# Pairing heads across the two groups on the partitions: landmark logits as 64-row, 32-column tiles, one scale for all heads

## Chip, cores, metric

One core of one Trainium2 chip. The metric is the device time of one execution in microseconds (us). The kernel before took 1018.75 us, the median of three runs.

## What is computed

Two stages. The first is landmark (Nystrom) attention with 8 batches, 8 heads, 576 tokens, 64 dimensions and 32 landmarks a head, the landmarks being means of 18 tokens:

```python
q_lm = q.reshape(B, H, 32, 18, D).mean(axis=3)      # k_lm the same from k
A  = softmax(scale * q    @ k_lm.T)                 # 576 x 32 a head
Bm = softmax(scale * q_lm @ k_lm.T)                 # 32 x 32
C  = softmax(scale * q_lm @ k.T)                    # 32 x 576
Z = Bm.T / (norm1(Bm) * norminf(Bm) + 1e-6)         # norms over the whole matrix
for _ in range(6): Z = 2 * Z - Z @ Bm @ Z
attn = A @ Z @ C @ v
```

The second takes x (batch, token, 512 columns of all heads), adds the real part of its two-dimensional Fourier transform over tokens and columns (u = x + mixed), normalises each token, and computes out = u + relu(un @ w_ch1) @ w_ch2 with 2048 hidden columns. All inputs are float32, w_ch1 and w_ch2 float64.

## The kernel before

Three threads of one program are woven into one order by a scheduler written out in the kernel (`run`, L930). Each thread is a Python generator that yields how long it wants to wait on a clock of estimates (`self.now`); whichever thread of the highest priority is due emits its next instructions. TensorE's order is thereby fixed by hand; the other engines' orders are left to the framework's scheduler, which goes by the order of emission and by free buffers. `attention` (priority 1) goes through the eight batches, `weights` (2) decodes the float64 weights and splits each into two fp16 halves, `mlp` (3) fills the rest: for each chunk of 256 tokens 192 hidden-layer matmuls (tile h) and 96 of the second layer (tile acc). Where nothing is due early on, filler matmuls are issued (L954).

Products that need more than fp16 are made as three fp16 matmuls (`mm3`: high x high, high x low, low x high) from a `split` of the operand (ScalarE writes the high half, VectorE the low). Small products stay in fp32.

The heads of a batch stand in two groups g of four. `load` (L360) brings k and q of group g as a tile of 128 partitions (two heads of 64 dimensions) by two pairs r. `tokens` (L382) sums the landmarks (lm), takes bounds of |q| and |k|, sets a scale for each group, and makes the logits of A: for each group a unit of four token tiles (u = 0, 1) and one unit (u = 2) for 64 remaining tokens. Since two heads share the 128 rows, each matmul's other operand (kbd) carries two heads' landmarks side by side with zeros in the wrong half (`mask2`). Softmax, the transposes of A, and the sums and differences over the heads of a group (F1, F2, Fh), which the transform needs, follow. `landmarks` (L536) is spawned as soon as lm is there. It makes the logits of B and C from the masked landmarks of q (qbd): for each group and pair an fp32 matmul of 128 rows by 64 columns, 32 columns wide for B (L551) and twice 288 wide for C (L589). Then come B's softmax and norms (nrm), the transposed C times v, six rounds of the iteration (RE, E), and the factors for `mix` (L725), which adds everything into u, from which `norm` and the MLP go on.

Four PSUM banks (`ps_at`, tile name at) serve all of the attention's matmuls in turn; `till(..., banks=n)` (L201) holds a thread back until the estimates say that n of them are free. SyncE issues all DMAs.

Of the kernel before, what the change touches and what calls it, by code (L numbers as in the profile page):

```python
# [131 lines left out]
class Kernel:  # L132
# [227 lines left out]
    def load(self, b):  # L360
# [4 lines left out]
        for g in range(2):  # L365
            kf, qf = self.big(), self.big()
            gs = slice(2 * g, 2 * g + 2)
            nc.sync.dma_start(kf[:, 0 : 2 * S].rearrange("p (r t) -> p r t", r=2), self.k[b, :, gs])
            nc.sync.dma_start(qf[:, 0 : 16 * SEG].rearrange("p (r t) -> p r t", r=2), self.q[b, :, gs])
# [12 lines left out]
    def tokens(self, b, st):  # L382
# [6 lines left out]
        lm = sm.tile([P, 2, 128], F32, name="lm", bufs=1)  # L389
        am = self.small(4, "amax")  # L390
        qbd = sm.tile([P, 4, 64], F32, name="qbd", bufs=1)
        qhs = []
        for g in range(2):
            kf, qf = loads[g][0][:, 0 : 2 * S], loads[g][1][:, 0:NQ]
            first = V.tensor_reduce(lm[:, g, 64:128], kf.rearrange("p (m t) -> p m t", t=18), AX.X, ALU.add)
# [3 lines left out]
            lv = lm[:, g, 0:64].rearrange("p (x o m) -> p x o m", o=2, m=8)  # L399
# [6 lines left out]
            A.activation(qhs[g][:, 0:NQ], qf, AF.Abs, accum_out=am[:, g : g + 1])  # L406
# [7 lines left out]
        st["loads"], st["qbd"], st["lm"] = loads, qbd, lm  # L414
        self.spawn(self.landmarks(b, st))

        eq, rq = self.power(am[:, 0:2], 2, 2.0**-13, "aq", b == 1)
        kb = self.small(2, "kb", BF16)
        V.tensor_tensor(kb, am[:, 2:4], eq, ALU.mult)
        yield self.till(kb, more=AM)  # L420
        ek, rk = self.bound(kb, 2, 2.0**-13, "ak")
        sc = self.small(4, "sc")
        V.tensor_tensor(sc[:, 0:2], eq, rk, ALU.mult)
        V.tensor_scalar(sc[:, 2:4], ek, 1.0 / 144.0, None, ALU.mult)
# [4 lines left out]
        for h2 in range(2):  # L429
            ms, cols = self.mask2[:, h2 : h2 + 1], slice(32 * h2, 32 * h2 + 32)  # L430
            V.tensor_scalar(
                kbd[..., cols].rearrange("p g y r m -> p (g y r) m"), klm.rearrange("p g y (r m) -> p (g y r) m", r=2),
                ms, None, ALU.mult,
            )
        qm = [h[:, 0:2048].rearrange("p (y r t) -> p y r t", y=2, r=2) for h in qhs]
        qr = [h[:, 2048:2304].rearrange("p (y r t) -> p y r t", y=2, r=2) for h in qhs]
        for g in range(2):
            qs = loads[g][1][:, 0:NQ].rearrange("p (x t) -> p x t", t=2 * SEG)
            for t, a, w in ((qm[g], 1, 128), (qr[g], 129, 16)):
                split(  # L440
                    *(t[:, y].rearrange("p r (s t) -> p (r s) t", t=w) for y in range(2)),
                    qs[:, :, a : a + w], rq[:, g : g + 1],
                )
            if g == 0:
                yield self.till(qhs[0], kbd)
# [3 lines left out]
        scr = self.small(1, "scr")  # L449
        for g in range(2):  # L450
            V.tensor_copy(scr[64 * g : 64 * g + 64], sc[64 * g : 64 * g + 64, 2 + g : 3 + g])
        aes = []
        for u in range(3):
            yield self.till(qhs[min(u, 1)])
            ps = self.psum()
            nh, scA = (16, sc[:, 2 + u : 3 + u]) if u < 2 else (4, scr)
            for j in range(4) if u < 2 else range(2):
                rows, at, g = (slice(0, P), 128 * j, u) if u < 2 else (slice(64 * j, 64 * j + 64), 0, j)
                for pr in range(2):
                    mm3(ps[rows, at + 64 * pr : at + 64 * pr + 64],  # L460
                        lambda y: qm[g][:, y, pr, 128 * j : 128 * j + 128] if u < 2 else qr[g][:, y, pr],
                        lambda y: kbd[:, g, y, pr, :])
# [7 lines left out]
            A.activation(ae, ae, AF.Exp, scale=scA)  # L470
# [7 lines left out]
        for u in range(3):  # L478
# [18 lines left out]
            if u < 2:  # L497

                F1, F2 = self.mid()[:, 0:512], self.mid()[:, 0:512]
                for x, op in enumerate((ALU.add, ALU.subtract)):  # L500
                    V.tensor_tensor(F1[:, 256 * x : 256 * x + 256], ae[:, 0:256], ae[:, 256:512], op)
                f1 = F1.rearrange("p (x k m) -> p x k m", x=2, k=2)
                for x, op in enumerate((ALU.add, ALU.subtract)):
                    (V if x == 0 else G).tensor_tensor(
                        F2[:, 256 * x : 256 * x + 256].rearrange("p (x m) -> p x m", x=2), f1[:, :, 0], f1[:, :, 1], op
                    )
            else:
                Fs.append(hl)
                break
            Fh = self.mid().bitcast(F16)[:, 0 : 2 * w].rearrange("p (y t) -> p y t", y=2)  # L510
            A.copy(Fh[:, 0], F2)
            G.tensor_tensor(Fh[:, 1], F2, Fh[:, 0], ALU.subtract)
            Fs.append(Fh)
        CS = self.big().bitcast(F16).rearrange("p (g y x t) -> p g y x t", g=2, y=2, x=2)
        for x in range(2):
            yield self.till(*Fs, banks=2)
            pss = [self.psum(), self.psum()]
            for g in range(2):
                for o in range(2):
                    i = (3, 0)[o] if x == 0 else (1, 2)[o]  # L520
                    mm3(pss[g][:, 160 * o : 160 * o + 160], lambda y: Fs[g][:, y, 128 * i : 128 * i + 128],
                        lambda y: self.t1[:, i, y, :], start=(o == 0), stop=False)
# [13 lines left out]
    def landmarks(self, b, st):  # L536
# [3 lines left out]
        loads, qbd, lm = st["loads"], st["qbd"], st["lm"]  # L540
# [11 lines left out]
        V.tensor_scalar(Bd.rearrange("p g m -> p (g m)"), ps[:, 0:64], 1.0 / 2592.0, None, ALU.mult)  # L552
# [23 lines left out]
        while b == 1 and self.seconds < NF // 2 - HB:  # L576
            yield 0.5

        for g in range(2):
            kv = loads[g][0][:, 0 : 2 * S].rearrange("p (r t) -> p r t", r=2)  # L580
# [443 lines left out]
```

## Time and profile before

| | |
|---|---|
| median of three runs | 1018.75 us (1017.17 to 1018.84) |
| profiled execution | 1018.43 us |
| its span, first to last instruction | 1016.6 us |
| TensorE busy | 969.0 us, 8407 matmuls |
| VectorE, ScalarE, POOL busy | 608.2, 335.5, 125.9 us |
| mean granted TensorE clock | 0.98 |

The profile shows one execution. Busy time of TensorE is pipelined, so matmul durations overlap; how long a piece of its stream takes is read from the start of its first instruction to the start of the next piece. An fp32 matmul of the program stands as two records. Batches are told apart by their first logits: B of batches 0 to 7 starts at 9.1, 131.4, 218.5, 326.2, 450.4, 555.1, 662.2 and 788.9 us.

### The profile page before, as it was taken

Reading aid. Unit: us, or ns where it says so; the run is one execution under the profiler, and the core shown is the slowest. Engines: PE = TensorE matmul, PEld = TensorE weight load, DVE = VectorE, ACT = ScalarE, POOL = GpSimd, SP = SyncE. Lnnn points to the kernel's source line nnn. Section 1 sums busy time; section 2 is a strip of 40 time slices with the busy share of each in tenths; the row PEclk is TensorE's granted clock in tenths of the full one; section 3 lists DMA queues with packets and bytes.
Section 4 is the critical chain, followed back from the end, with each engine's and each line's share of the span. In section 5 each row is a group of like instructions: output and inputs, shape, how many; then the busy total and the mean of one; then the engine's idle time right before and its main releaser. Section 6 shows DMA issues by size and latency. Waiting matters only on the chain.

```text
span 1016.6 us, 20320 instructions
## 1 busy us (share of the span) xinstructions
PE 969.0 (95%) x8407; PEld 673.3 (66%) x8407; DVE 608.2 (60%) x1654; ACT 335.5 (33%) x723; POOL 125.9 (12%) x144
## 2 busy tenths in 40 slices
PE   5776989999999999999999999999999999999998
PEld 3654756667776676666766776667676676666665
DVE  6979797786655855287556855686453834351111
ACT  4658653343223322142233323332212322111110
POOL 0000000013011400024011401122020220110000
PEclk8887999999999999999999999999999999999999
DMA  9863204142312240112402240225020200120000
GB/s 328 254 250 111 83 2 167 22 71 51 148 21 45 43 164 11 43 36 53 161 12 53 50 168 6 58 48 180 1 53 11 58 15 22 22 53 21 1 22 21
DMA packets 97772, 74.63 MB, mean 73 GB/s; under 512 B 68112, under 2 KB 86544, under 8 KB 97552
## 3 DMA queue, kind: packets, MB, share of 16 engines
q1 hardware_dynamic: 97680, 73.34, 24.7%
q8 instruction: 66, 1.08, 0.5%
q14 instruction: 26, 0.21, 0.1%
HBM read 48.02 MB, written 9.44 MB: 57 GB/s over the span
## 4 chain that ended last, share of the span: by engine, by line
PE 82%; DVE 11%; ACT 3%; DMA 2%; issue 1%; POOL 1%; SPq 0%; DVEq 0%; POOLq 0%; ACTq 0%
PE h L210 34%; PE acc L210 34%; PE at L210 13%; DVE w L127 2%; DVE mid L127 1%; ACT mid L127 1%; DMA mid<-mid 1%; DVE lm L127 1%; DVE cmx L127 1%; DVE asum L127 1%; DMA big<-q_dram 1%; DMA big<-k_dram 1%; POOL mid L127 1%; PE at L215 1%; DVE amx L127 0%
## 5 line engine op out<-in xcount | busy, mean ns | idle before, releaser
L210 PE MATMUL h<-unT,w 128*128 128x256 f16 x3456 | 411.2, 273 | 0.0
L210 PEld LDWEIGHTS <-w 128*128 128x128 f16 (+1 forms) x3584 | 346.2, 99 | 73.2 <-issue 3.3
L210 PE MATMUL acc<-w,h 128*128 128x512 f16 x1680 | 394.3, 380 | 0.0
L210 PEld LDWEIGHTS <-h 128*128 128x128 f16 x1680 | 161.8, 98 | 161.9 <-issue 4.4
L127 DVE SCALAR_TENSOR_TENSOR h<-h 128x512 f16<-128x512 f32 x140 | 96.1, 687 | 198.7 <-ACT h L127 198.0
L127 ACT ACTIVATE h<-h 128x512 f16<-128x512 f32 x140 | 83.2, 595 | 308.0 <-PE h L210 295.8
L127 POOL TENSOR_TENSOR r<-ve,mhalf 128x2 f32<-128x2 f32 (+1 forms) x20 | 13.7, 685 | 411.1 <-DVE ve L127 404.1
L127 POOL TENSOR_TENSOR mid<-mid 128x640 f16<-128x640 f32 (+2 forms) x36 | 40.9, 1144 | 114.2 <-ACT mid L127 107.9
L127 DVE TENSOR_TENSOR mid<-mid 128x256 f32<-128x256 f32 (+2 forms) x68 | 45.3, 682 | 13.2 <-DMA mid<-mid 9.4
L127 DVE TENSOR_REDUCE lm<-big 128x32 f32<-128x576 f32 (+1 forms) x48 | 44.2, 946 | 10.2 <-DMA big<-k_dram 9.5
L127 DVE SCALAR_TENSOR_TENSOR u<-at,scw,row 128x128 f32<-128x128 f32 (+3 forms) x120 | 38.6, 389 | 13.8 <-PE at L210 11.8
L210 PEld LDWEIGHTS <-big 128*128 128x128 f16 (+1 forms) x768 | 39.7, 101 | 10.2 <-issue 2.8
L210 PEld LDWEIGHTS <-mid 64*128 64x128 f16 (+1 forms) x624 | 30.0, 96 | 18.8 <-issue 8.6
L127 ACT CAST row<-row 128x512 f16<-128x512 f32 (+1 forms) x40 | 20.7, 551 | 62.7 <-DVE row L127 62.7
L127 DVE SCALAR_TENSOR_TENSOR row<-at,scw,row 128x262 f32<-128x262 f32 (+1 forms) x48 | 21.3, 486 | 28.3 <-ACT row L127 21.4
L127 POOL TENSOR_TENSOR row<-row 128x512 f16<-128x512 f32 (+1 forms) x33 | 34.3, 1055 | 30.7 <-ACT row L127 28.8
L210 PE MATMUL at<-RE,E 128*128 128x96 f32 (+1 forms) x192 | 30.5, 281 | 4.3 <-DVE RE L127 4.3
L127 DVE SCALAR_TENSOR_TENSOR u<-acc,wsc,u 128x512 f32<-128x512 f32 x36 | 26.8, 749 | 12.5 <-PE acc L210 11.8
L210 PEld LDWEIGHTS at<-RE,E 128*128 128x128 f32 x192 | 27.1, 194 | 10.6 <-DVE RE L127 4.4
L210 PE MATMUL at<-mid,big 128*128 128x262 f16 (+1 forms) x288 | 31.8, 279 | 0.0
L127 DVE SCALAR_TENSOR_TENSOR big<-big,aq_r 128x1024 f16<-128x1024 f32 (+1 forms) x32 | 26.8, 868 | 3.9 <-ACT big L127 3.9
L127 ACT CAST mid<-mid 128x512 f16<-128x512 f32 (+1 forms) x28 | 18.1, 671 | 28.2 <-POOL mid L127 20.5
(166 smaller groups left out, 928.6 us busy)
## 6 DMA issues: line engine op xcount, KB each, us to landing
w<-w_dram SPq DMA_DIRECT2D x22, 512.0 KB, 8.7
big<-v_dram SPq DMA_DIRECT2D x16, 640.0 KB, 8.9
big<-q_dram SPq DMA_DIRECT2D x16, 584.0 KB, 6.0
big<-k_dram SPq DMA_DIRECT2D x16, 576.0 KB, 5.0
out_dram<-u SPq DMA_DIRECT2D x36, 256.0 KB, 2.0
big<-w_dram SPq DMA_DIRECT2D x10, 512.0 KB, 6.8
t<-t_dram SPq DMA_DIRECT2D x1, 1048.0 KB, 9.2
unT<-row SPq DMA_TRANSPOSE x64, 2.5
```

Source lines behind the costliest of these rows:

```text
L127: return call(out, *args, **kw)
L210: self.nc.tensor.matmul(out, a, b, start=start, stop=stop, skip_group_check=True)
L215: self.nc.tensor.transpose(out, a, ident)
```

## The change

Heads are paired across the groups: partitions 0 to 63 carry the heads of group 0, 64 to 127 those of group 1; the four heads of a group stand as two tiles e by two columns o. Each tile of k or q now comes by two DMAs of 64 partitions. One scale serves all heads. Landmarks of q need no mask: a head's B and C are matmuls of its own 64 rows by 32 columns, so eight small tiles cover the array, and both groups' B and C go into four banks, B behind the first half of C. The remaining 64 tokens of A become 24 matmuls of 32 columns in place of 12 of 64. The sums over heads are taken between the two units of A, and so stand behind both.

```diff
 load():
-            gs = slice(2 * g, 2 * g + 2)
-            nc.sync.dma_start(kf[...], self.k[b, :, gs])
-            nc.sync.dma_start(qf[...], self.q[b, :, gs])
-            for t in (kf, qf):
+            for t, src, n in ((kf, self.k, S), (qf, self.q, 8 * SEG)):
+                for half in range(2):
+                    nc.sync.dma_start(
+                        t[64 * half : 64 * half + 64, 0 : 2 * n].rearrange("p (o t) -> p o t", o=2),
+                        src[b, :, 2 * half + g].rearrange("(o p) t -> p o t", o=2),
+                    )
 tokens():
-            for h2 in range(2):
-                ms, cols = self.mask2[:, h2 : h2 + 1], slice(32 * h2, 32 * h2 + 32)
-                V.tensor_scalar(
-                    qbd[:, 2 * g : 2 * g + 2, cols], lm[:, g, 0:64].rearrange("p (r m) -> p r m", r=2), ms, None, ALU.mult
-                )
-            yield self.till(qbd)
-        V.tensor_reduce(am[:, 2:4], lm[:, :, 64:128], AX.X, ALU.max, apply_absolute_value=True)
+            yield self.till(lm)
+        V.tensor_reduce(km, lm[:, 1].rearrange("p e m -> p (e m)"), AX.X, ALU.max, apply_absolute_value=True)
...
-        eq, rq = self.power(am[:, 0:2], 2, 2.0**-13, "aq", b == 1)
+        V.tensor_tensor(qs, am[:, 0:1], am[:, 1:2], ALU.add)
+        eq, rq = self.power(qs, 1, 2.0**-13, "aq", b == 1)
...
-        for g in range(2):
-            split(klm[:, g, 0], klm[:, g, 1], lm[:, g, 64:128], sc[:, g : g + 1])
+        split(*(klm[:, y].rearrange("p e m -> p (e m)") for y in range(2)), lm[:, 1].rearrange("p e m -> p (e m)"), sc[:, 0:1])
...
-        scr = self.small(1, "scr")
-        for g in range(2):
-            V.tensor_copy(scr[64 * g : 64 * g + 64], sc[64 * g : 64 * g + 64, 2 + g : 3 + g])
...
+            if u < 2:
+                pt = ps.rearrange("p (j g r m) -> p j g r m", j=2, g=2, r=4)
+                for j in range(2):
+                    for r in range(4):
+                        at = 128 * (2 * u + j)
+                        mm3(pt[:, j, :, r], lambda y: qm[r // 2][:, y, r % 2, at : at + 128], lambda y: kbd[:, y, r // 2, r % 2].rearrange("p (g m) -> p g m", g=2))
+            else:
+                for r in range(4):
+                    for g in range(2):
+                        mm3(ps[64 * g : 64 * g + 64, 32 * r : 32 * r + 32], lambda y: qr[r // 2][:, y, r % 2],
+                            lambda y: kbd[:, y, r // 2, r % 2, 32 * g : 32 * g + 32])
...
+        F1 = [self.mid()[:, 0:512] for _ in range(2)]
+        for x, op in enumerate((ALU.add, ALU.subtract)):
+            V.tensor_tensor(F1[x], aes[0], aes[1], op)
+        for x, op in enumerate((ALU.add, ALU.subtract)):
+            F2 = self.mid()[:, 0:512]
+            for k in range(2):
+                (V if x == 0 else G).tensor_tensor(F2[:, 256 * k : 256 * k + 256], F1[k][:, 0:256], F1[k][:, 256:512], op)
 landmarks():
-        ps = self.psum()
-        for g in range(2):
-            for pr in range(2):
-                mm(ps[64 * pr : 64 * pr + 64, 32 * g : 32 * g + 32], qbd[:, 2 * g + pr], lm[:, g, 64 + 32 * pr : 96 + 32 * pr])
+        yield self.till(lm, banks=4)
+        heads = [(slice(64 * g, 64 * g + 64), slice(32 * r, 32 * r + 32), g, r // 2, r % 2) for r in range(4) for g in range(2)]
+        halves = [[self.psum() for g in range(2)] for hf in range(2)]
+        for half, row, g, e, o in heads:
+            mm(halves[0][g][row, 288:320], lm[half, 0, e, 32 * o : 32 * o + 32], lm[half, 1, e, 32 * o : 32 * o + 32], share=0.3)
+        for hf in range(2):
+            for half, row, g, e, o in heads:
+                kv = loads[e][0][half, S * o + 288 * hf : S * o + 288 * hf + 288]
+                mm(halves[hf][g][row, 0:288], lm[half, 0, e, 32 * o : 32 * o + 32], kv, share=0.21)
+        for g in range(2):
+            V.tensor_scalar(Bd[:, g], halves[0][g][:, 288:320], 1.0 / 2592.0, None, ALU.mult)
...
-                for pr in range(2):
-                    mm(ps[64 * pr : 64 * pr + 64, 0:288], qbd[:, 2 * g + pr], kv[:, pr, 288 * hf : 288 * hf + 288])
-                V.tensor_reduce(cmx[:, hf : hf + 1], ps[:, 0:288], AX.X, ALU.max)
+                V.tensor_reduce(cmx[:, hf : hf + 1], halves[hf][g][:, 0:288], AX.X, ALU.max)
```

The order of instructions moves with it. TensorE, batch 7, where B and C stand between hidden-layer matmuls (h from unT and w). Before:

```order
L210 LDWEIGHTS h
L210 MATMUL acc_9657<-w_74,h 128x512
L210 LDWEIGHTS w_73
L210 MATMUL h<-unT,w_73 128x256
...
L210 MATMUL at<-lm,qbd 64x32 x4
L210 MATMUL at<-big,qbd 64x288 x8
```

and of the change:

```order
L210 LDWEIGHTS h
L210 MATMUL acc_9809<-w_74,h 128x512
L210 LDWEIGHTS w_73
L210 MATMUL h<-unT,w_73 128x256
...
L210 MATMUL at<-lm 32x32 x8
L210 MATMUL at<-big,lm 32x288 x16
```

Between the last acc and B stand 12 hidden-layer matmuls before and 6 now; the count of small matmuls doubles. Behind C, before the matmul with ones for the norms (nrm), stand 12 (batch 2) or 15 (batches 3 and 7) MLP matmuls before, and 30 now; the bound matmul kb stands right behind nrm before, and ahead of it now, after 24 to 30 MLP matmuls in batches 2 to 7.

VectorE, the same place of batch 7: u from at are the last adds of batch 6, Bd, bmx and bs B's softmax, cmx and cb the maxima of C. Before:

```order
L127 SCALAR_TENSOR_TENSOR u<-acc_9656,wsc,u 128x512
L127 SCALAR_TENSOR_TENSOR u<-acc_9657,wsc,u 128x512
L127 TENSOR_SCALAR Bd<-at 128x64
L127 TENSOR_REDUCE bmx<-Bd 128x2
L127 SCALAR_TENSOR_TENSOR u<-at,scw,row 64x256
L127 SCALAR_TENSOR_TENSOR u<-at,scw,row 64x128 x2
L127 TENSOR_TENSOR Bd<-Bd,bmx 128x64
L127 TENSOR_REDUCE cmx<-at 128x1
```

and of the change:

```order
L127 SCALAR_TENSOR_TENSOR u<-acc_9808,wsc,u 128x512
L127 SCALAR_TENSOR_TENSOR u<-acc_9809,wsc,u 128x512
L127 SCALAR_TENSOR_TENSOR u<-at,scw,row 64x256
L127 SCALAR_TENSOR_TENSOR u<-at,scw,row 64x128 x2
L127 TENSOR_SCALAR Bd<-at 128x32 x2
L127 TENSOR_REDUCE cmx<-at 128x1
L127 TENSOR_REDUCE bmx<-Bd 128x2
L127 TENSOR_REDUCE cmx<-at 128x1
```

The adds of the batch before now stand ahead of the first reading of B.

VectorE, the start of the program: lm are the sums of landmarks (64 wide of k, 4x8 of q), w_73 the weights. Before:

```order
L127 TENSOR_REDUCE lm<-big 128x64
L127 TENSOR_REDUCE lm<-big 128x4x8 x2
L127 TENSOR_SCALAR qbd<-lm,mask 128x2x32 x2
L127 TENSOR_REDUCE lm<-big 128x64
L127 TENSOR_REDUCE amax<-lm 128x2
L127 TENSOR_REDUCE lm<-big 128x4x8 x2
L127 TENSOR_SCALAR qbd<-lm,mask 128x2x32 x2
L127 TENSOR_SCALAR w_73<-w_74 128x512
```

and of the change:

```order
L127 TENSOR_REDUCE lm<-big 128x64
L127 TENSOR_REDUCE lm<-big 128x4x8 x2
L127 TENSOR_REDUCE lm<-big 128x64
L127 TENSOR_REDUCE kmax<-lm 128x1
L127 TENSOR_REDUCE lm<-big 128x4x8 x2
L127 TENSOR_SCALAR w_73<-w_74 128x512
L127 SCALAR_TENSOR_TENSOR w_73<-row,w_73 128x512
```

The two pairs of masks are gone from the first instructions, and the sums follow each other.

## Rows read from the trace of the kernel before

**Rows 1.** The page: busy time of TensorE (us, share of the span, instructions), and the shares of the chain that ended last, by engine.

```profile
PE 969.0 (95%) x8407; PEld 673.3 (66%) x8407; DVE 608.2 (60%) x1654; ACT 335.5 (33%) x723; POOL 125.9 (12%) x144
...
PE 82%; DVE 11%; ACT 3%; DMA 2%; issue 1%; POOL 1%; SPq 0%; DVEq 0%; POOLq 0%; ACTq 0%
```

**Rows 2.** Busy time of the engines by stretch: the stretch and its length, busy us and instructions of each engine, granted TensorE clock, busy share of the DMA engines, GB/s.

```profile
0.00:125.00 125.00, 91.97 (x873) 70.46 (x874) 101.45 (x272) 80.90 (x163) 5.02 (x12) 0.85 0.61 208
125.00:250.00 125.00, 117.71 (x1123) 80.17 (x1122) 103.65 (x304) 50.30 (x112) 16.68 (x20) 0.99 0.25 60
250.00:950.00 700.00, 696.60 (x5994) 481.63 (x5993) 392.54 (x1065) 197.76 (x438) 104.20 (x113) 1.00 0.21 57
```

**Rows 3.** The chain that ended last, from 0 to 130 us: start, length (us), what. The second row is B and C of batch 0.

```profile
12.01 0.43 DVE qbd L127 x2
12.48 2.81 PE at L210 x16
```

**Rows 4.** TensorE in order of time, batch 2: start, time to the end of the last (us), what, how many; in brackets an idle time and what ended it.

```profile
218.50 0.43 PE L210 MATMUL at<-lm,qbd 128*64 128x32 f32 x8
218.76 2.14 PE L210 MATMUL at<-big,qbd 128*64 128x288 f32 x16
220.83 1.47 PE L210 MATMUL acc<-w,h 128*128 128x512 f16 x6
```

**Rows 5.** The same, batch 7: C (transposed) times v in 80 records on strips of 32 columns, then 24 logits of A and the 12 of the remainder, and a round of the iteration on the full array.

```profile
806.18 1.73 PE L210 MATMUL at<-big,mid 128*32 128x64 f32 x80
807.84 1.27 PE L210 MATMUL at<-kbd,big 128*128 128x64 f16 x36
809.04 1.47 PE L210 MATMUL acc<-w,h 128*128 128x512 f16 x6
810.35 0.58 PE L210 MATMUL at<-RE,E 128*128 128x96 f32 x4
810.76 0.81 PE L210 MATMUL acc<-w,h 128*128 128x512 f16 x3
```

**Rows 6.** The same, in batch 2's mix: fp16 matmuls on 64 rows, the two halves in turn.

```profile
292.44 0.84 PE L210 MATMUL at<-Wx,mid 64*128 64x128 f16 x24
293.21 1.47 PE L210 MATMUL acc<-w,h 128*128 128x512 f16 x6
```

**Rows 7.** The chain that ended last in batch 7: 24 hidden-layer matmuls of 256 columns, and 24 logits of A of 64.

```profile
797.07 2.62 PE h L210 x24
...
800.99 0.70 PE at L210 x24
```

**Rows 8.** All engines in order of time around B and C of batch 7.

```profile
787.18 1.63 SPq L883 DMA_DIRECT2D out_dram<-u  x2
...
788.90 0.42 PE L210 MATMUL at<-lm,qbd 128*64 128x32 f32 x8
...
789.16 2.36 PE L210 MATMUL at<-big,qbd 128*64 128x288 f32 x16
...
789.77 0.98 DVE L127 SCALAR_TENSOR_TENSOR u<-at,scw,row 64x256 f32<-64x256 f32 x3
...
790.81 0.44 DVE L127 TENSOR_REDUCE cmx<-at 128x1 f32<-128x288 f32 x1
...
791.45 1.49 PE L210 MATMUL h<-unT,w 128*128 128x256 f16 x12
```

**Rows 9.** What TensorE waited for from 200 us on: who, us in total, times, the longest.

```profile
PE at L210 <- ACT mid L127: 1.0, 2, 0.5
PE at L210 <- DVE nrm L127: 0.7, 1, 0.7
```

**Rows 10.** VectorE's instructions by shape: output and inputs, count | busy us, mean ns of one | idle time before them and what ended it.

```profile
L127 DVE TENSOR_REDUCE asum<-mid 128x16 f32<-128x512 f32 x16 | 10.9, 683 | 3.9 <-ACT mid L127 3.8
...
L127 DVE TENSOR_SCALAR qbd<-lm,mask 128x64 f32<-128x64 f32 x32 | 6.9, 248 | 0.1
...
L127 DVE SCALAR_TENSOR_TENSOR klm<-lm,sc,klm 128x64 f16<-128x64 f32 x16 | 5.2, 352 | 0.6 <-ACT klm L127 0.4
...
L127 DVE TENSOR_TENSOR E<-at,mask 128x256 f32<-128x256 f32 x40 | 16.6, 415 | 7.7 <-PE at L210 7.5
...
L127 DVE COPY scr<-sc 64x1 f32<-64x1 f32 x16 | 2.3, 144 | 0.1
...
L127 DVE TENSOR_SCALAR Bd<-at 128x64 f32<-128x64 f32 x8 | 1.8, 221 | 4.6 <-PE at L210 4.5
```

**Rows 11.** All engines in order of time, batch 1.

```profile
133.83 0.31 PE L210 MATMUL at<-lm,qbd 128*64 128x32 f32 x4 [2.16 <-DVE qbd L127]
...
137.51 0.16 PE L210 MATMUL at<-kb,ones 128*128 128x2 bf16 x1 [1.40 <-ACT mid L127]
```

**Rows 12.** SyncE's issues in order of time at the start: start, time, what.

```profile
1.19 0.42 SPq L368 DMA_DIRECT2D big<-k_dram  x1
1.66 0.42 SPq L369 DMA_DIRECT2D big<-q_dram  x1
```

**Rows 13.** All engines in order of time, batch 1 near its end.

```profile
169.87 1.35 DVE L127 TENSOR_REDUCE lm<-big 128x64 f32<-128x1152 f32 x1 [1.90 <-DMA big<-k_dram]
...
172.36 0.41 PE L210 MATMUL at<-RE,Bbd 128*128 128x64 f32 x2 [1.63 <-DVE RE L127]
```

**Rows 14.** ScalarE in order of time, batch 7: the first exponential of C.

```profile
793.46 0.49 ACT L127 ACTIVATE mid<-at,cb 128x288 f32<-128x288 f32 x1
```

More of the change, by code (lines that the diff above doesn't have):

```diff
@@ L388, in tokens @@
         NQ = 16 * SEG
-        lm = sm.tile([P, 2, 128], F32, name="lm", bufs=1)
-        am = self.small(4, "amax")
-        qbd = sm.tile([P, 4, 64], F32, name="qbd", bufs=1)
+        lm = sm.tile([P, 2, 2, 64], F32, name="lm", bufs=1)
+        am = self.small(2, "amax")
         qhs = []
-        for g in range(2):
-            kf, qf = loads[g][0][:, 0 : 2 * S], loads[g][1][:, 0:NQ]
-            first = V.tensor_reduce(lm[:, g, 64:128], kf.rearrange("p (m t) -> p m t", t=18), AX.X, ALU.add)
+        for e in range(2):
+            kf, qf = loads[e][0][:, 0 : 2 * S], loads[e][1][:, 0:NQ]
+            first = V.tensor_reduce(lm[:, 1, e], kf.rearrange("p (m t) -> p m t", t=18), AX.X, ALU.add)
             if b == 1:
                 self.tc.keep_in_program_order(first)
-            lv = lm[:, g, 0:64].rearrange("p (x o m) -> p x o m", o=2, m=8)
+            lv = lm[:, 0, e].rearrange("p (x o m) -> p x o m", o=2, m=8)
             qv = qf.rearrange("p (x o t) -> p x o t", o=2, t=2 * SEG)
@@ L414, in tokens @@
-        st["loads"], st["qbd"], st["lm"] = loads, qbd, lm
+            A.activation(qhs[e][:, 0:NQ], qf, AF.Abs, accum_out=am[:, e : e + 1])
+            yield self.till(lm)
+        kb = self.small(2, "kb", BF16)
+        km, qs = self.small(1, "kmax"), self.small(1, "qsum")
+        V.tensor_reduce(km, lm[:, 1].rearrange("p e m -> p (e m)"), AX.X, ALU.max, apply_absolute_value=True)
+        st["loads"], st["lm"] = loads, lm
         self.spawn(self.landmarks(b, st))
-        eq, rq = self.power(am[:, 0:2], 2, 2.0**-13, "aq", b == 1)
@@ L418, in tokens @@
-        kb = self.small(2, "kb", BF16)
-        V.tensor_tensor(kb, am[:, 2:4], eq, ALU.mult)
+        V.tensor_tensor(qs, am[:, 0:1], am[:, 1:2], ALU.add)
+        eq, rq = self.power(qs, 1, 2.0**-13, "aq", b == 1)
+        V.tensor_tensor(kb[:, 0:1], km, eq, ALU.mult)
         yield self.till(kb, more=AM)
[L421 to L424, printed above, removed]
+        ek, rk = self.bound(kb, 1, 2.0**-13, "ak")
@@ L429, in tokens @@
-        for h2 in range(2):
-            ms, cols = self.mask2[:, h2 : h2 + 1], slice(32 * h2, 32 * h2 + 32)
             V.tensor_scalar(
-                kbd[..., cols].rearrange("p g y r m -> p (g y r) m"), klm.rearrange("p g y (r m) -> p (g y r) m", r=2),
-                ms, None, ALU.mult,
+                kbd[..., 32 * g : 32 * g + 32].rearrange("p y e r m -> p (y e r) m"), klm.rearrange("p y e (r m) -> p (y e r) m", r=2),
+                self.mask2[:, g : g + 1], None, ALU.mult,
             )
@@ L436, in tokens @@
         qr = [h[:, 2048:2304].rearrange("p (y r t) -> p y r t", y=2, r=2) for h in qhs]
-        for g in range(2):
[L438 to L445, printed above, removed]
+        for e in range(2):
+            qs = loads[e][1][:, 0:NQ].rearrange("p (x t) -> p x t", t=2 * SEG)
+            for t, a, w in ((qm[e], 1, 128), (qr[e], 129, 16)):
+                split(*(t[:, y].rearrange("p r (s t) -> p (r s) t", t=w) for y in range(2)), qs[:, :, a : a + w], rq)
@@ L496, in tokens @@
             st["AT"].append(AT)
[L497 to L510, printed above, removed]
+        F1 = [self.mid()[:, 0:512] for _ in range(2)]
[5 more added lines that the diff above has]
+                (V if x == 0 else G).tensor_tensor(F2[:, 256 * k : 256 * k + 256], F1[k][:, 0:256], F1[k][:, 256:512], op)
+            Fh = self.mid().bitcast(F16)[:, 0:1024].rearrange("p (y t) -> p y t", y=2)
             A.copy(Fh[:, 0], F2)
@@ L584, in landmarks @@
             csum, cmx = self.small(2, "csum"), self.small(2, "cmx")
-            halves = []
             for hf in range(2):
-                ps = self.psum()
-                for pr in range(2):
-                    mm(ps[64 * pr : 64 * pr + 64, 0:288], qbd[:, 2 * g + pr], kv[:, pr, 288 * hf : 288 * hf + 288])
-                V.tensor_reduce(cmx[:, hf : hf + 1], ps[:, 0:288], AX.X, ALU.max)
-                halves.append(ps)
+                V.tensor_reduce(cmx[:, hf : hf + 1], halves[hf][g][:, 0:288], AX.X, ALU.max)
             cb = self.small(1, "cb")
```

35 lines of the change are left out of this document (15 added, 20 removed).

## The prediction

> **What bounds the kernel now.** I read the page first: TensorE is busy for 969.0 of 1016.6 us and holds 82% of the chain that ended last [rows 1]. An average hides stages, so the second view is the table by stretch [rows 2]. Up to 125 us TensorE is busy for 92.0 (partly filler matmuls) at a mean granted clock of 0.85, while VectorE, which decodes the weights, has 101.5. From 125 to 250 us TensorE misses 7.3 us. From 250 to 950 us it misses 3.4 of 700, at the full clock. So two rules hold. After 250 us a microsecond of TensorE work removed is a microsecond of the run, one of waiting is a microsecond added, and work taken from VectorE is worth nothing unless TensorE waits for it. Before about 140 us the chain runs through VectorE's instructions [rows 3, 11], and there VectorE's work counts.
>
> The profiled execution took 1018.43 us, its span is 1016.6; the median of three runs is 1018.75. I sum against 1018.43, 0.3 under that median. A measurement of this kernel can tell about 0.2% (2 us) from no change.
>
> **The logits of B and C.** In a later batch they are one piece of TensorE's stream: in batch 2 from 218.50 to 220.83 us, 2.33 us, of which B is the first 0.26 and C 2.07 [rows 4]. An fp32 matmul shows as two records, so C's 16 records of 288 columns run at 0.259 us a pair, two column strips side by side. The change has 32 records of the same length, each on 64 rows by 32 columns. If all eight places of the array work at once, that is 4 rounds of 0.259 = 1.04 us; if only four do, 8 rounds = 2.07, no gain. The rows have both halves of this packing, never together. Four strips of 32 columns: 80 fp32 records of 64 columns take 1.66 us, 21 ns each, where 4 full-array records of 96 columns take 0.41 us, 102 ns each, by proportion 68 for 64 columns: 3.3 at a time [rows 5]. Two row halves: 24 fp16 matmuls of 128 columns in 0.77 us, 32 ns each [rows 6], where the full array takes 109 for 256 columns [rows 7], so 55: 1.7 at a time. The product, 5.6 of 8, makes 1.49 us, a pessimistic end, since the change of shape at either end of those short pieces weighs less under 288 columns. I take 1.2, nearer to the full packing. The Trainium skill (TensorE: Matmul & The Clock Gate, Part 3) reports 10.6 times for 16 tiles packed both ways. By that share, an estimate, C takes 1.04 x 16/10.6 = 1.57 us, and the sum below is 1.5 us worse. B goes from 8 records to 16; at 21 ns it takes 0.33. Together 2.33 becomes 1.53: -0.8 us, for batches 2, 4, 5 and 6 **-3.2**.
>
> **Four banks at once.** Before, C's last quarter reused B's bank, and the first maxima were taken while C still ran. Now B and C fill all four banks of the pool, and no other small matmul can run until the exponentials free them. In batch 7 (and 3, which stands alike) that meets a late reader: the last adds of the batch before (u, from banks of mix) start only at 789.77, after the output transfers issued from 787.18 on, and end at 790.75. Already before, C lost time there, 2.29 us from its start to the next h where batch 2 took 2.07 [rows 4, 8]. Now TensorE arrives 6 hidden-layer matmuls (0.65 us) sooner, at 788.25, has the first half of C done by about 789.2, and waits for the adds until 790.25 to 790.75; then 0.6 us for the second half. That ends at 790.85 to 791.35, against 791.45 - 0.65 = 790.8 before: +0.4 each, **+0.8**. In return the plan lays 30 MLP matmuls between C and the ones-matmul of the norms in batches 2, 3 and 7, 12 to 15 before. TensorE's waits for ScalarE and nrm there, 1.0 and 0.7 us [rows 9], should mostly go; but the hold is longer (first rival), and I book **-0.5**.
>
> **The logits of A.** The two big units keep 24 full-array matmuls of 64 columns each, with an output in two pieces: nothing. The remainder goes from 12 matmuls of 64 columns to 24 of 32. Before, 36 took 1.20 us [rows 5] and 24 took 0.70 [rows 7], so 12 cost 0.50. They pay mostly for weights of 64 columns each, which halving the moving width leaves alone. Bounds: +0.1 (the two strips overlap) to +0.5 (each costs what it did); I take +0.2, since the strips are independent. The Trainium skill (TensorEngine Tiling, Instruction Overhead) speaks against this part: a matmul of one column has the latency of one of 60, so no factor is to be had from a dimension that is already short. By that, an estimate, 24 cost twice what 12 did, +0.5, and the sum is 2.1 us worse. No row shows fp16 matmuls of 32 columns yet. For seven batches after the first: **+1.4**.
>
> **VectorE.** Per batch go four masks of q (0.248 each), one of two splits of k (0.352; the other, twice as wide, grows by an estimated 0.05) and two copies of 0.144; the first sums over heads become two of 512 columns (0.68, as asum's over 512) in place of four of 256 (0.415, as E's over 256) [rows 10]. Added are one more scaling of B (0.22) and one sum of maxima (an estimated 0.15). That is -0.99 - 0.30 - 0.29 - 0.30 + 0.37 = -1.5 us. In batches 2 to 7 this is worth nothing. In batch 0 the masks of the second half (0.43) and C at 2.81 us, under a low clock, stand in the chain [rows 3]. Against them the loads: each of SyncE's first transfers occupies it 0.42 us and the next starts 0.46 later [rows 12]; each becomes two, so q of the first half is issued 0.9 us later, and lands later by nothing (the bytes being the limit) to 0.9. VectorE is 81% busy in those 125 us, so weights fill most gaps. I take **-1.0** for batch 0 (bounds -2.5 and +1). In batch 1 TensorE waited 2.16 us for the mask of q, then 1.40 for ScalarE's exponentials [rows 11]: two masks and some scalars leave the chain ahead of it, the hold of the banks stays. **-1.0** (bounds -2 and +1).
>
> In batch 1 TensorE also waited 1.63 us for RE, whose add stood in VectorE's queue behind the first sum of batch 2; that sum had waited 1.90 us for k [rows 13]. The doubled transfers make k later by up to 0.5, a place ahead of the output transfers makes it earlier: 0, between -1.6 and +0.5. POOL and ScalarE do nearly the same work, and the plan lays the matmuls that need the sums over heads later.
>
> **Sum:** -3.2 + 0.8 - 0.5 + 1.4 - 1.0 - 1.0 = -3.5 us: **1014.9 us**, 0.4% under the median. With all good ends (C at 1.04: -0.6; remainder +0.1: -0.7; no wait in batches 3 and 7: -3.2; the start: -2.5; RE: -1.6) it is 1006.3; with 1.49 for C and +0.5 for the remainder it is 1014.9 + 1.5 + 2.1 = 1018.5.
>
> **Rivals.**
> - *The banks decide (slower).* The place is the bound matmul kb, the first to need a bank after C. In batch 7 C ended at 791.45, the first exponential at 793.95, with the first maximum taken before C's end [rows 4, 8, 14]. Now all four maxima (0.45 each) come after C, and the first bank comes free some 3 to 4 us after it, while the plan leaves 24 to 30 MLP matmuls, 3.9 us. Whenever a relu or an add cuts in on either engine, TensorE pays the excess. At 1.4 us in each of six batches that is 8.4: 1023.3. It decides from 0.6 us a batch, where the 3.5 are gone. For it: the waits of [rows 9] were this very wait. Against: twice as many matmuls cover it now. Chance 0.14.
> - *The row halves take turns (no change).* If fp32 tiles on the two halves do not run together, C stays at 2.07 and B near 0.4: the -3.2 becomes +0.6, batches 3 and 7 cost 0.5 more each: 1014.9 + 3.8 + 1.0 = 1019.7. For it: no fp32 row has both halves. Against: the fp16 rows do [rows 6]. Chance 0.13.
> - *It does only part of what it is to do (no change).* The start gains nothing, since the weights set it and the doubled transfers eat the masks, and the remainder costs 0.4: 1014.9 + 2.0 + 1.4 = 1018.3. Chance 0.15.
> - *More than that.* Half of the good ends: 1010.6. Chance 0.12.
>
> **Chances and range.** The forecast with its own range, 1012.5 to 1017.5, has 0.46. Faster by over 0.2% (under 1016.7): most of the forecast, the good ends, a bit of the third rival: 0.58. Slower (over 1020.8): most of the first rival and the upper part of the second: 0.16. The same: 0.26. The range of 1008.5 to 1020.5 takes in the good ends' middle and the second and third rivals, and leaves out the first.
>
> **What would show it.** After the change: B and C in batch 2 in about 1.5 us (2.1 or more: the halves take turns); a wait of 1 to 1.6 us inside C in batches 3 and 7 for an add to u; 0.6 to 1.0 us for the remainder of A; no mask ahead of the first C; at most 0.3 us of waiting at kb and the norms in batches 2 to 7. Waits at kb in most batches, less done by 250 us than before, or TensorE's idle time growing by what its busy time loses would make the forecast wrong.

## The result, and the profile after

The change made the kernel slower: 1024.81 us (median of 5 runs, 1022.71 to 1026.59) against 1018.84, a ratio of 1.0057 with a 95% interval of 1.0038 to 1.0075. The forecast was 1014.9 us. The profiled execution took 1026.59 us, the longest of the five; its span is 1024.8.

The page: TensorE's busy time, and the chain that ended last.

```profile
PE 965.4 (94%) x8710; PEld 669.7 (65%) x8710; DVE 599.3 (58%) x1598; ACT 336.0 (33%) x715; POOL 125.8 (12%) x144
...
PE 67%; DVE 10%; issue 10%; DMA 6%; POOL 2%; ACT 2%; SPq 1%; POOLq 0%; DVEq 0%; ACTq 0%
```

Against [rows 1] TensorE is busy for 3.6 us less, as hoped; but the rest of the span grew from 47.6 to 59.4 us. By stretch:

```profile
0.00:125.00 125.00, 88.27 (x913) 69.09 (x914) 99.95 (x268) 81.49 (x163) 4.70 (x12) 0.85 0.68 208
125.00:250.00 125.00, 113.80 (x1160) 75.29 (x1158) 102.66 (x288) 49.57 (x109) 17.58 (x21) 0.97 0.25 60
250.00:950.00 700.00, 692.33 (x6169) 479.13 (x6168) 384.69 (x1027) 197.23 (x431) 103.52 (x111) 1.00 0.25 57
```

Against [rows 2] TensorE misses 3.7 us more up to 125 us (filler matmuls count as busy there), 3.9 more in the second stretch, at a lower granted clock, and 4.3 more in the third. What it waited for from 200 us on (who, us in total, times, longest):

```profile
PE at L210 <- DVE RE L127: 7.8, 7, 2.5
PE at L210 <- DVE u L127: 1.6, 2, 0.8
PE acc L210 <- DVE u L127: 0.9, 1, 0.9
```

and for RE before, from the view of [rows 9]:

```profile
PE at L210 <- DVE RE L127: 2.0, 2, 1.6
```

The waits of [rows 9] for ScalarE's exponentials and nrm are gone; those for RE have grown from 2.0 to 7.8 us. They stand in batches 2, 3, 4, 5 and 7.

**B and C did what was wanted.** TensorE in order of time, batch 2:

```profile
217.56 0.27 PE L210 MATMUL at<-lm 64*32 64x32 f32 x13
...
217.66 1.16 PE L210 MATMUL at<-big,lm 64*32 64x288 f32 x29
218.76 2.76 PE L210 MATMUL acc<-w,h 128*128 128x512 f16 x12
```

From 217.56 to 218.76 it is 1.20 us where [rows 4] have 2.33.

**In batch 5, TensorE before**, where the logits of A (at from kbd and big) of the two units stand 24 h and 9 acc apart:

```profile
565.30 0.86 PE L210 MATMUL at<-kbd,big 128*128 128x64 f16 x24
566.00 2.78 PE L210 MATMUL h<-unT,w 128*128 128x256 f16 x24
568.62 2.11 PE L210 MATMUL acc<-w,h 128*128 128x512 f16 x9
570.56 0.86 PE L210 MATMUL at<-kbd,big 128*128 128x64 f16 x24
```

**and after:** all 72 stand in one piece, TensorE then waits 2.54 us for RE, and the 12 acc behind the wait take 4.24 us to the next piece, where at the full clock 12 take 2.6. The last row is the granted clock there (last column but two), 0.66. In the 5 us around the waits of 1.0 us in batches 3 and 4 it was 1.00.

```profile
572.47 2.06 PE L210 MATMUL at<-kbd,big 128*128 128x64 f16 x72
...
582.10 0.36 PE L210 MATMUL at<-RE,E 128*128 128x96 f32 x2
585.00 0.46 PE L210 MATMUL at<-RE,E 128*128 128x96 f32 x2 [2.54 <-DVE RE L127]
585.30 4.44 PE L210 MATMUL acc<-w,h 128*128 128x512 f16 x12
589.54 2.71 PE L210 MATMUL h<-unT,w 128*128 128x256 f16 x23
```

```profile
585.00:590.00 5.00, 5.00 (x18) 2.25 (x19) 3.93 (x6) 1.74 (x4) 4.80 (x6) 0.66 0.32 66
```

VectorE and POOL there, after:

```profile
583.82 0.87 DVE L127 TENSOR_TENSOR mid<-mid 128x512 f32<-128x512 f32 x1 [1.95 <-POOL mid L127]
584.62 0.33 DVE L127 TENSOR_SCALAR RE<-at,cr,ci 128x64 f32<-128x64 f32 x1
```

```profile
581.63 1.15 POOL L127 TENSOR_TENSOR row<-mid,row 128x512 f16<-128x512 f32 x1 [0.73 <-ACT row L127]
582.74 1.05 POOL L127 TENSOR_TENSOR mid<-mid,asum 128x512 f32<-128x512 f32 x1
```

The first sum over heads (mid from mid, 583.82) reads both units, so it waits for POOL to normalise the second (582.74); POOL did the subtraction of the first unit before that; and RE, for which TensorE waits, stands behind the sum in VectorE's queue.

**Batch 1, TensorE after**, and the granted clock behind kb (last column but two):

```profile
135.36 0.23 PE L210 MATMUL at<-lm 64*32 64x32 f32 x4 [1.41 <-DVE lm L127]
...
139.91 0.16 PE L210 MATMUL at<-kb,ones 128*128 128x1 bf16 x1 [3.31 <-ACT mid L127]
139.94 4.00 PE L210 MATMUL acc<-w,h 128*128 128x512 f16 x9
143.73 2.53 PE L210 MATMUL h<-unT,w 128*128 128x256 f16 x12
```

```profile
140.00:145.00 5.00, 5.00 (x16) 2.15 (x16) 4.02 (x24) 3.73 (x10) 0.00 (x0) 0.50 0.00 0
```

kb waited 1.40 us in [rows 11], now 3.31; and the granted clock behind it is 0.50, the lower level (1.2 of 2.4 GHz). Nine acc at 1.95 and twelve h at 1.31 at the full clock take 3.79 and 2.36: some 2.9 us more, beside the 1.9 of the wait.

### The profile page after: what moved, and what is told of

It is laid out like the page before. It is cut to its first block, busy times and chain, and to the rows that moved or that the text cites. A ratio compares the mean times of both kernels' runs of the same rounds, so it can differ in the third digit from the quotient of the medians.

```text
span 1024.8 us, 20948 instructions
## 1 busy us (share of the span) xinstructions
PE 965.4 (94%) x8710; PEld 669.7 (65%) x8710; DVE 599.3 (58%) x1598; ACT 336.0 (33%) x715; POOL 125.8 (12%) x144
## 4 chain that ended last, share of the span: by engine, by line
PE 67%; DVE 10%; issue 10%; DMA 6%; POOL 2%; ACT 2%; SPq 1%; POOLq 0%; DVEq 0%; ACTq 0%
PE h L210 28%; PE acc L210 28%; PE at L210 10%; DMA w<-w_dram 3%; DVE mid L127 2%; DVE w L127 2%; POOL mid L127 1%; DMA mid<-mid 1%; DMA big<-q_dram 1%; DVE u L127 1%; DVE asum L127 1%; SPq L634 1%; ACT mid L127 1%; DVE h L127 1%; ACT row L127 1%
## 5 line engine op out<-in xcount | busy, mean ns | idle before, releaser
L127 DVE TENSOR_TENSOR mid<-mid 128x256 f32<-128x256 f32 (+3 forms) x52 | 39.6, 794 | 17.0 <-POOL mid L127 8.5
L127 ACT ACTIVATE big<-big,aq_r 128x1024 f16<-128x1024 f32 (+1 forms) x32 | 23.4, 775 | 10.6 <-DVE aq_r L127 10.6
```

What stands on the lines that cost most here:

```text
L127: return call(out, *args, **kw)
```

## The experiments

The theory after this comparison had three losses (the doubled transfers, kb in batch 1, the sums ahead of RE). Ratios are to the kernel before on the same chip; 0.001 is 1.02 us; the change stands at 1.0057.

**1. Whole transfers** in the change, the heads reordered on the host to give the same tiles:

```diff
-                for half in range(2): nc.sync.dma_start(t[64 * half : 64 * half + 64, ...], src[b, :, 2 * half + g]...)
+                nc.sync.dma_start(t[:, 0 : 2 * n]..., src[b, :, 2 * g : 2 * g + 2])
```

> The change with k and q loaded as before, four transfers of 128 rows (the heads are laid out on the host in an order that gives the same tiles), nothing else undone. Theory (three losses: the eight half transfers hold SyncE's queue 1.3 us a pair and delay all weights; the bound matmul kb of batch 1 stands right behind C; the sums over heads stand ahead of RE on VectorE): SyncE's first weight transfer is issued near 3.3 us again (6.51 in the change) and the time falls by 2 to 3 us, to about 1022.3. Rival 1 (the weights' decoding on VectorE sets the start, the later issue is hidden): 1024.8, within 1. Rival 2 (the doubled transfers eat all that the start lost): 1020 or less.

1021.91 us, 1.0032 (1.0014 to 1.0051): 2.5 us less, as the theory had it, though the interval overlaps that of the change (1.0038 to 1.0075).

**2. kb of batch 1 later:**

```diff
         yield self.till(kb, more=AM)
+        if b == 1:
+            yield 3.5
```

> The change with 3.5 us of hidden- and output-layer matmuls planned between C and the bound matmul kb in batch 1 alone. Theory: the wait of 3.3 us for ScalarE at kb goes and so does the stretch at the low clock behind it (about 3.3 us lost): the time falls by 3 to 5 us, to about 1021. Rival 1 (the chain through VectorE and ScalarE to A's first matmul is what counts in batch 1, and later kb only moves the wait to A): no fall, 1024.8 within 1, with a wait of 2 to 3 us for A's operands. Rival 2 (the clock falls anyway, from the waits of batch 0 or RE): -1.5 to -2, about 1023.

1020.71 us, 1.0019 (1.0008 to 1.0030): 3.9 us less, as forecast. The wait and the low clock at kb went, but TensorE waited later in batch 1:

```profile
138.99 0.46 PE L210 MATMUL at<-nrm,ones_bd 128*128 128x128 f32 x2 [1.46 <-DVE nrm L127]
...
151.96 0.66 PE L215 MATMUL at<-ident,mid 128*128 128x128 f32 x4 [2.42 <-POOL mid L127]
```

**3. The sums later** (`if b > 0: yield 3.0` ahead of F1):

> The change with the sums over heads of A emitted 3 us of matmuls later in every batch but the first, so that the adds to RE stand ahead of them in VectorE's queue. Theory: TensorE's waits for RE after 200 us (7.8 us in 7) fall below 2, and the time falls by 4 to 6 us, to about 1020. Rival 1 (the waits move to the matmuls that read the sums, which now come later): TensorE's waits for ScalarE's or POOL's mid grow by 2 us or more and the time falls by less than 2, 1023 to 1025. Rival 2 (RE is late for the normalising on POOL itself, not for the place of the sums): the waits for RE stay.

1032.66 us, 1.0140 (1.0114 to 1.0166). The edit missed its aim: only TensorE's order goes by the yields, VectorE's is the framework's, and in batch 3 the sum still stood ahead of RE and waited 1.95 us for POOL, as without it (1.96). It decides nothing on its theory. Why 8 us more is open; the six runs' mean granted clock was 0.969 to 0.976.

**4. The three together:**

> The three edits together (whole loads, the bound matmul of batch 1 later, the sums over heads later). Theory: what they win adds up, 9 to 13 us, and the kernel ends between 1012 and 1016, faster than before (1018.8) by the 3 to 6 that B and C lost. Rival (the waits exchange places: when one goes, the next one in the same batch ends last): the sum is under two thirds of the parts, 1017 or more, no faster than before.

1023.97 us, 1.0049 (1.0033 to 1.0066): the rival's outcome, but the third edit alone had cost 8 us. Two of them without the third:

> The change with whole transfers and with the bound matmul of batch 1 later, the two edits that were each worth something alone (2.5 and 3.9 us). Theory (independent losses, one before 125 us, one at 136 to 150 us): both count in full, 1024.8 - 2.5 - 3.9 = 1018.4, the same as before. Rival (with data earlier, the waits of batch 1 grow again by what the start wins): 1020.5 or more.

1023.55 us, 1.0054 (1.0035 to 1.0074). Edits worth 2.5 and 3.9 us were worth 0.3 together. TensorE in batch 1, with both:

```profile
140.37 0.77 PE L210 MATMUL at<-nrm,ones_bd 128*128 128x128 f32 x2 [2.14 <-DVE nrm L127]
154.77 1.12 PE L215 MATMUL at<-ident,mid 128*128 128x128 f32 x4 [2.42 <-POOL mid L127]
```

With the transfers whole, TensorE waits for nrm 2.14 us where it waited 1.46 with kb's edit alone. So the losses are not separate: the theory of three fell.

**5. POOL out of the way of the sums:** `self.G if b > 0 else V` became `self.G if b > 0 and u != 1 else V` for the normalising.

> The change with the normalising of A's second unit on VectorE instead of POOL in batches 1 to 7, nothing else. Theory (the first sum over heads now reads both units, stands ahead of an add to RE in VectorE's queue and waits there 2 us for POOL's second normalising, which comes behind POOL's subtraction of the first unit's halves): TensorE's waits for RE after 200 us, 7.8 us in 7, fall below 3 and the time by 4 to 5 us, to about 1020. Rival 1 (RE is late for its own chain or for the longer sums, not for POOL): the waits stay, 1024 to 1026. Rival 2 (VectorE's 0.7 us more a batch make another wait): TensorE waits for another tile of VectorE as long as it did for RE, 1023 to 1026.

1023.31 us, 1.0048 (1.0031 to 1.0066). TensorE's waits for RE after 200 us fell from 7.8 to 4.4 us, so POOL is part of it; the time fell by 0.9 us where 4 to 5 were forecast, which the two intervals can't tell from nothing. These runs had a lower mean granted clock, 0.970 to 0.978 against 0.975 to 0.980: at 0.977 and 0.978 they took 1021.7 and 1020.5 us, where the change at 0.977 took 1024.2 and 1025.1. So a gain may be hidden by the clock; why that was lower is open.

**6. The transfers alone, in the kernel before**, cut by rows as in the change, and by head pair on all 128 rows:

```diff
-            nc.sync.dma_start(kf[...], self.k[b, :, gs])
+            for half in range(2): nc.sync.dma_start(t[hs, ...], src[b, hs, gs])   # 64 rows
+            for r in range(2): nc.sync.dma_start(t[:, n * r : n * r + n], src[b, :, 2 * g + r])   # the other kernel
```

> The kernel before with each of the transfers of q and k cut in two by rows of SBUF (64 partitions each), as the change does, nothing else. Theory (eight issues of 0.63 us hold SyncE's queue and the weights behind it): first weight transfer issued near 6.5 us instead of 3.3, time +2 to +3 us, 1021 to 1022. Rival (the start of the change is late for its own chain, not for the loads): +0.5 or less.

> The kernel before with each of the transfers of q and k cut in two by head pair (128 partitions each, half the bytes of a row), so as many transfers as in the change but on all rows. If the number of issues is what costs: as with the halves by rows, SyncE's queue is held 0.6 us by each, the first weights are issued near 6.5 us, +2 to +3 us. If it is that a transfer covers only 64 rows: each issue takes 0.42 us or less, the first weights are issued by 5 us, and the time is within 1 us of before.

1019.08 us, 1.0009 (1.0000 to 1.0019), and 1018.20, 1.0006 (0.9992 to 1.0019). SyncE's issues by half rows and by head pairs, two a row:

```profile
2.42 1.24 SPq L371 DMA_DIRECT2D big<-q_dram  x2
...
6.25 1.14 SPq L347 DMA_DIRECT2D w<-w_dram  x2
```

```profile
2.12 0.91 SPq L370 DMA_DIRECT2D big<-q_dram  x2
...
4.97 1.54 SPq L347 DMA_DIRECT2D w<-w_dram  x2
```

A transfer on 64 rows holds SyncE for 0.62 us, one of as many bytes on 128 rows for 0.45, and a whole one 0.42 [rows 12]. So it is the 64 rows that hold SyncE longer. The weights, issued at 6.25 us in place of 3.31, cost the kernel before 0.9 us (0 to 1.9 by the interval), not 2 to 3; and the intervals of the two kernels overlap, so that the time itself doesn't tell rows from head pairs.

**7. The units of A apart.** The order of instructions shows what the theory lacked: before, unit 0 waited for one half of q and unit 1 for the other; with heads paired across the groups each unit needs both, and the matmuls between them are gone in batches 1 to 7. In the change, and its reverse in the kernel before:

```diff
+            if u == 1 and b > 0:      # the change, nothing else
+                yield 2.6
...
-            yield self.till(qhs[min(u, 1)])
+            yield self.till(*qhs)      # the kernel before, nothing else
```

> The change with 2.6 us of hidden- and output-layer matmuls planned between the first and the second big unit of A in batches 1 to 7, nothing else. In the kernel before, unit 0 needed one half of q and unit 1 the other, and the plan laid 24 such matmuls between them; in the change each unit has heads of both halves, and the two stand back to back in every batch. Theory (the bunching makes three softmaxes pile up on VectorE and POOL ahead of the adds to RE and of the transposes): TensorE's waits for RE from 200 us on fall from 7.8 us to under 3, and the time by 3 to 6 us, to about 1020. Rival 1 (the sums' wait for POOL is what matters, and unit 1 only comes later): waits for RE stay within 2 us, 1024 to 1026. Rival 2 (all of the loss lies before 150 us): waits fall but the time falls by under 1.5.

1016.31 us, 0.9974 (0.9962 to 0.9987): 8.5 us under the change, where 3 to 6 were forecast, and faster than before. Batch 5 and the waits from 200 us on:

```profile
569.25 0.86 PE L210 MATMUL at<-kbd,big 128*128 128x64 f16 x24
569.95 2.75 PE L210 MATMUL acc<-w,h 128*128 128x512 f16 x12
...
573.20 1.35 PE L210 MATMUL at<-kbd,big 128*128 128x64 f16 x48
...
580.16 0.89 PE L210 MATMUL at<-RE,E 128*128 128x96 f32 x4 [0.47 <-DVE RE L127]
```

```profile
PE acc L210 <- DVE u L127: 2.1, 1, 2.1
PE at L210 <- DVE u L127: 1.6, 2, 0.8
PE at L210 <- DVE RE L127: 0.8, 2, 0.5
```

The wait for RE went from 2.54 us to 0.47 here, from 7.8 to 0.8 in all. The code of the sums and of POOL is as it was, but VectorE's order is not: both adds to RE now stand ahead of the first sum, and that waits 0.29 us for POOL in place of 1.95:

```profile
579.76 0.34 DVE L127 TENSOR_SCALAR RE<-at,cr,ci 128x64 f32<-128x64 f32 x1
...
580.19 0.34 DVE L127 TENSOR_SCALAR RE<-at,cr,ci 128x64 f32<-128x64 f32 x1
...
581.48 0.87 DVE L127 TENSOR_TENSOR mid<-mid 128x512 f32<-128x512 f32 x1 [0.29 <-POOL mid L127]
```

The second rival's place for the loss (before 150 us) is out: up to 250 us the change and this kernel both have 2073 matmul records behind them, so the gain lies later.

> The kernel before with both big units of A planned only when both halves of q are split, as the change needs it, nothing else: the 24 matmuls between the two units go, as in the change. Theory (bunching is a loss of its own): waits for RE, asum and POOL's mid appear as in the change, and the time rises by 3 to 6 us, to 1022 to 1025. Rival (the loss comes from the sums over heads, which here still read one unit each, or from the banks at kb): within 1.5 us of before.

1021.58 us, 1.0032 (1.0020 to 1.0043): the bunching alone costs the kernel before 3.3 us. There it shows in batch 1 most:

```profile
185.21 0.53 PE L210 MATMUL at<-t,Wt 128*64 128x262 f16 x6 [3.35 <-DVE Wx L127]
185.67 3.66 PE L210 MATMUL h<-unT,w 128*128 128x256 f16 x18
```

```profile
185.00:190.00 5.00, 4.79 (x31) 3.41 (x31) 3.44 (x11) 0.98 (x2) 0.00 (x0) 0.66 0.00 0
```

At the same place the kernel before waits 0.81 us, at the full clock. TensorE's waits for RE from 200 us on, which the theory said would appear, did not: 2.1 us, as before (2.0). So bunching alone does not make RE late. In the change, where the first sum also reads both units, it does, and undoing the bunching gives 8.5 us. That the sums make this difference fits the batch shown, but no run has the change with sums that read one unit each. How the bunching leads to the wait at 185 us was not followed.

**8. What is left, one by one on top of the units apart.**

> The change with the units of A apart and kb of batch 1 later by 3.5 us. Theory (kb's wait of 3.3 us and the low clock behind it are a loss of their own): 3 to 4 us under the kernel with the units apart alone (1016.3), 1012.5 to 1013.5. Rival (batch 1 moves its wait to the next wait in it, as with whole transfers and kb together): within 1.5 us of 1016.3.

1011.70 us, 0.9932 (0.9915 to 0.9949): 4.3 us for kb in batch 1.

> The change with the units of A apart and whole transfers. If the half transfers cost what they cost in the kernel before: 0.9 us less than 1016.3. If what they cost in the change: 2.5 less, 1013.8. If what they cost beside the four edits: 6 less, about 1010. Rival (an earlier start only lengthens the wait at kb in batch 1): within 1 us of 1016.3.

1015.64 us, 0.9968 (0.9956 to 0.9979): 0.6 for the transfers, which the intervals can't tell from nothing; kb then waited 3.97 us, the rival's wait.

> The four edits of the plan without the one at kb of batch 1 (units apart, unit 1 normalised on VectorE from batch 2 on, B and C of batches 3 and 7 later by 1.2 us). Theory (the waits for u inside C, 1.6 us in two, go, and what is left of the waits for RE, 0.8 us): 2 to 3 us under 1016.3, 1013.3 to 1014.3; kb is then worth 4 to 5 of the four edits. Rival (the wait for u only moves to the next reader of the banks): 1015.5 or more.

1013.56 us, 0.9948 (0.9933 to 0.9964): 2.7 for u's banks in batches 3 and 7 and unit 1's normalising.

**9. All of the plan's edits (those of 2 and 7 and the two below), without and with whole transfers:**

```diff
+        yield self.till(lm, banks=4, more=1.2 if b in (3, 7) else 0.0)   # B and C
+            (self.G if b > 0 and not (b > 1 and u == 1) else V).tensor_tensor(...)   # normalising
```

> The change with four edits of the plan: kb of batch 1 later by 3.5 us, units of A apart by 2.6 us, unit 1 normalised on VectorE from batch 2 on, B and C of batches 3 and 7 later by 1.2 us (so that u's banks are free). Theory (the losses lie in TensorE's waits at kb, RE and u, 3.3 + 7.8 + 1.6 us of waiting and 1.7 us more at the low clock than before, while B and C give 1.1 us a batch): all the waits after 200 us go but 2 us, the time is 1012 to 1016, faster than before. Rival (batch 1 and the start lose whatever the plan): 1018 to 1021.

> The four edits of the plan and whole transfers of q and k. Theory (the halves cost what they cost in the kernel before, 0.9 us): 0.5 to 1.5 us under the kernel with the four edits alone. Rival 1 (2.5 us, as the edit alone gave in the change): 2 to 3 us under it. Rival 2 (an earlier start only moves the waits of batch 1, as with the two edits together): no gain, or slower by up to 3.

1009.24 us, 0.9911 (0.9889 to 0.9933), where the parts of 8 add up to 0.9906 (1012 to 1016 us were forecast); and 1002.80, **0.9850** (0.9831 to 0.9869), a version 15 us faster than the kernel before. By stretch, with whole transfers:

```profile
125.00:250.00 125.00, 119.84 (x1245) 82.66 (x1245) 99.45 (x289) 48.97 (x110) 16.54 (x21) 0.99 0.26 74
250.00:950.00 700.00, 698.64 (x6220) 484.62 (x6219) 387.68 (x1030) 196.19 (x430) 101.68 (x105) 1.00 0.21 55
```

TensorE misses 5.2 us in the second stretch and 1.4 in the third, against 7.3 and 3.4 before [rows 2]. These edits thus also take out waiting that the kernel before has. No run gives that kernel such edits, so how much of the 15 us is due to the new pairing is not shown. That whole transfers gave 6.2 us here, more than any of the three cases above, and 0.6 on top of the units apart stays open. The mean granted clock was 0.982 or more in each of these runs and 0.974 to 0.981 in those with half transfers: at 0.981 two of the latter took 1005.8 and 1005.9 us, at 0.982 three of the former 1002.2 to 1005.2, so more than half of the 6.2 may go with the clock.

## Why the prediction was wrong

**The step that failed** is "The logits of A. The two big units keep 24 full-array matmuls of 64 columns each, with an output in two pieces: nothing." The matmuls did keep their number and cost: all of A takes 1.99 us in batch 5 (572.47 to the next piece), against 0.70 + 0.80 + 0.39 in its three pieces before. What went was the 24 and more MLP matmuls between the units, through a dependence (both halves of q for each unit, qm[r // 2] in the diff) that the sum never priced: a term of nothing stood where 8.5 us were lost. With the units apart again the time is 1016.3, inside the 1012.5 to 1017.5 of the likeliest case. That it lies there is partly luck: it still holds the loss at kb below, and a wait for u of 2.1 us that no term had, and B and C save more than was booked. Nor is it to the first rival's credit that its 1023.3 lies near 1024.81: its waits, at kb in six batches, did not come.

**The same error in "the plan lays the matmuls that need the sums over heads later":** it looked at who reads the sums, and not at what queues behind them on VectorE, which is RE. RE was priced for batch 1 (at 0) and in no other, and the 7.8 us stand in later ones. That the sum stands ahead of RE and waits 1.95 us there is read from the trace of batch 5 (1.96 in batch 3); experiment 3, which was to prove it, did not move the sum.

**Batch 1, booked at -1.0 with bounds of -2 and +1:** "the hold of the banks stays" was wrong. Before, the first maxima were taken while C ran; now all four follow it, and nothing stands between C and kb there. By the two profiles that is +1.9 of waiting and +2.9 behind it, less 0.75 ahead of B (1.41 against 2.16 for the mask) and a wait of 0.53 at the norms that is gone: some +3.5, beyond the upper bound. Moving kb gives back 4.3 us by experiment 8. It is the first rival's mechanism, not in the six batches for which it was priced, but in batch 1.

**Right in kind:**
- B and C -0.8 a batch: -1.1 measured (1.20 against 2.33). C's 32 records take 1.1 us, near the 1.04 of eight places at once. The Trainium skill (TensorE: Matmul & The Clock Gate, Part 3) gives 10.6 for 16 tiles of 32 by 32; carried over to these tiles, that made an estimated 1.57; this trace does not agree with it. The rival that the row halves take turns is out.
- The remainder of A, +0.2: some +0.1, by the 1.99 against 1.89. The doubling estimated from the Trainium skill (TensorEngine Tiling (Array Packing), Instruction Overhead), +0.5, is not seen in this trace.
- Batches 3 and 7: a wait inside C for u, 0.80 us in batch 7, was forecast in place and cause (1 to 1.6 us).

```profile
795.85 0.27 PE L210 MATMUL at<-lm 64*32 64x32 f32 x13
...
797.42 1.23 PE L210 MATMUL at<-big,lm 64*32 64x288 f32 x16 [0.80 <-DVE u L127]
798.59 2.14 PE L210 MATMUL h<-unT,w 128*128 128x256 f16 x18
```

From B to the next h it is 2.74 us against 2.55 [rows 8]: +0.2 for a forecast +0.4.
- The waits of the norms, and kb in batches 2 to 7: none are left, as forecast; the first rival is out for those.
- The doubled transfers: the first weights are issued 3.2 us later (6.51 against 3.31). That cost 0.9 us in the kernel before and 0.6 beside the units apart, within the bound of +1 on batch 0, and neither clear of zero; whole transfers gave 2.5 in the change itself and 6.2 beside all the edits, beyond it.

**Open:** batch 0, booked at -1.0. B of batch 1 starts at 133.69 us after and at 131.36 before, but in the eight profiles with the change's code up to there it starts at 131.26 to 135.86, on average 133.4, and in the five with whole transfers at 127.73 to 132.50, on average 129.9. So the halves cost some 3.6 us at that place, beyond the bound, but with this spread a term of 1 us can't be read off; and how much of it reaches the end differs, as above. And one bound was added up wrongly: 1.49 for C costs 1.2 us in four batches, not 1.5, so that end is 1018.2; nothing hangs on it.

The text named what would make it wrong, "TensorE's idle time growing by what its busy time loses": busy -3.6, the rest +11.8.

## What to carry to other kernels

When data are regrouped, list for each piece of work which inputs it now waits for, beside what it costs: work that could be staggered by halves becomes one burst when every piece needs both halves, and a burst on the engines off the critical path can delay whatever is queued behind it there. The order of instructions shows this before any run: look for filler that used to separate two pieces and doesn't any more. And where edits that each gain do not add up, look for a common cause upstream. Here it was found for the waits; the worth of whole transfers still went from 0.6 to 6.2 us with what stood beside them.

## What the runs showed of the hardware that was not expected

- Eight fp32 tiles of 64 rows by 32 columns run together at nearly the full count: 32 records of 288 columns in 1.1 us, 35 ns each.
- A wait of TensorE can cost more than its length. Behind 3.31 us at kb the granted clock was 0.50 over 5 us; behind 3.35 at 185 us, in the kernel before with the units bunched, and behind 2.54 in batch 5 it was 0.66. It doesn't always come: the same wait of 2.12 us for u in batch 2 was followed by 12 acc in 4.44 us in one profile (units apart, the first row below) and in 2.75 in another (the plan's edits without kb's, the second). The runs of one kernel spread with their mean granted clock: with whole transfers alone, those at a mean granted clock of 0.980 took 1019.2 to 1019.5 us, those at 0.973 to 0.975 took 1026.2 to 1026.8.

```profile
231.63 4.44 PE L210 MATMUL acc<-w,h 128*128 128x512 f16 x12 [2.12 <-DVE u L127]
...
231.55 2.75 PE L210 MATMUL acc<-w,h 128*128 128x512 f16 x12 [2.12 <-DVE u L127]
```

- A transfer of k or q on 64 rows held SyncE for 0.62 us, longer than one of twice the bytes on 128 rows (0.42).
